# A cubic with one VectorE pass fewer for the offloaded exponentials, with 68 packs instead of 65 and new plan constants, in a gated mix of softmax attention and linear attention

## The chip, the cores and the metric

The kernel runs on one core of one Trainium2 chip. The metric is the device time of one execution in microseconds (us). Most executions of a kernel agree within about 0.3%. Each run also lists the mean clock that TensorE was granted (1.000 is full speed). The *span* is the time from the first to the last instruction of the execution that was profiled.

Engines: PE is TensorE (matmuls), PEld its weight loads, DVE is VectorE, ACT is ScalarE, POOL is GpSimd, SP the engine that issues most transfers.

## The reference

```python
x = A_x                                    # [1, 2048, 512] bf16
g = sigmoid((x * gate_w).sum(-1, keepdims=True))
a = softmax_attention(x, A_wqkv, A_wo)     # 32 heads of 16: softmax(q k^T / 4) v, then @ wo
b = hedgehog_linear_attention(x, B_wqkv, B_w_phi, B_wo)   # features: softmax over 16, of +pq and of -pq
return g * a + (1 - g) * b
```

What costs the time is the softmax attention. It needs exp() of 32 x 2048 x 2048 scores. Four heads' scores of 128 keys by 512 queries are four *units* of 128x512. There are 2048 units.

## The kernel before

The program builds a list of operations with dependences and estimated durations. A scheduler inside the kernel source orders them for each engine, and the result is a fixed instruction order per engine. Changing a constant of the plan changes that order, and with it how many spare matmuls the scheduler puts in to keep TensorE active (103 in before).

The heads are processed in 32 steps (`n`), each of 16 key tiles (`kt`) of four units. ScalarE does the exponentials of most key tiles, out of PSUM into the tile `ET`. Some key tiles, `dve_tiles(n)`, are given to VectorE and GpSimd instead. One such tile is a *pack* of four units, computed with integer tricks and a polynomial.

```python
LEAD = [16.9408, 8.9394, 19.7683, 21.1253, 20.1566]      # plan constants: how early
PACE = [7.9948, 0.4589]                                   # work is released, and when
BOUNDS = [5.8136, 10.5124, 10.0461, 26.2873]              # the linear branch runs
EM = 53
EPHI = 0.49984589
E1, E2, E3 = 125.48413, 43.840203, 9.9574722
DVE_COUNT = (1, 1, 1, 2, 2, 2, 2, 1, 3, 2, 1, 3, 1, 2, 3, 1,      # packs of each step: 65
             2, 3, 2, 2, 2, 2, 3, 2, 1, 3, 2, 2, 4, 1, 3, 3)
# ...
TICK, QUOTA = 3.413, 3700      # spare matmuls keep TensorE active while it has nothing to do
# ...
    def dve_pack(self, n, kt, first_pv):
        # ... four score matmuls into ps_mp, each evacuated by VectorE:
            ws.append(s.op("dve", 0.605, lambda e, i=i, b=b: e.tensor_scalar(
                self.EW[...], self.bk(b), float(EC), float(127 * 65536), op0=ALU.mult, op1=ALU.add), ...))
        # ... integer half on GpSimd, fraction half on VectorE:
        h = s.op("pool", 1.9, lambda e: e.tensor_scalar(
            out().bitcast(dt.int16), half(1, dt.int16), 128.0, float(EM), op0=ALU.mult, op1=ALU.add), ws, ...)
        f = s.op("dve", 1.13, lambda e: e.tensor_scalar(
            self.Ef[:], half(0, dt.uint16), float(2.0 ** -16), -EPHI, op0=ALU.mult, op1=ALU.add), ...)
        t = s.op("dve", 0.6, lambda e: e.tensor_scalar(
            self.Em[:], self.Ef[:], E3, E2, op0=ALU.mult, op1=ALU.add), [f], ...)
        u = s.op("dve", 1.13, lambda e: e.tensor_tensor(self.Em[:], self.Ef[:], self.Em[:], ALU.mult), [t], ...)
        q = s.op("dve", 0.6, lambda e: e.tensor_scalar(self.Em[:], self.Em[:], E1, None, op0=ALU.add), [u], ...)
        g_ = s.op("dve", 1.13, lambda e: e.tensor_tensor(self.Em[:], self.Ef[:], self.Em[:], ALU.mult), [q], ...)
        vs = [s.op("dve", 1.13, lambda e: e.tensor_tensor(out(), out().bitcast(dt.int16), self.Em[:], ALU.add), [g_, h], ...)]
        # ... the pack's four matmuls with V add into the step's accumulator ps_ot
```

Two waits in the main chain tie ScalarE to the packs:

```python
            if ub - NSLOT >= 0:                       # ET has 15 slots: an exponential waits
                deps.append(self.o_pv[(ub - NSLOT) // 4])   # for the matmul that frees its slot
            # ...
                if kt == NT - 1:                      # the step's closing matmul waits for
                    deps += dpv[n]                    # all packs of the step
```

So a pack that comes late delays the closing matmul of its step. The matmuls behind it wait in order, the slots of `ET` fill, and ScalarE stops.

The softmax here doesn't subtract the row's maximum and nothing guards it: scores larger than these inputs give would overflow.

## Time and profile before

| | before |
|---|---|
| time, median of 3 runs | 871.35 us (870.81 to 872.87) |
| span of the profiled run | 871.1 us, granted clock 0.988 |
| ScalarE busy | 842.7 us (97%) |
| VectorE busy | 796.9 us (91%) |
| GpSimd busy | 131.5 us (15%) |

The page gives the busy time of each engine, then the chain of work that ended last, then groups of instructions: line, engine, operation, output<-input, shapes, count, and after the bar the busy time in us, the mean ns of one, and the engine's idle time just before them with what ended most of it. L735 is the exponential on ScalarE. L825 and L828 are the two cheap polynomial passes, L827 a tensor-by-tensor pass.

```profile
PE 748.0 (86%) x5242; PEld 215.5 (25%) x5330; DVE 796.9 (91%) x1118; ACT 842.7 (97%) x783; POOL 131.5 (15%) x76
...
ACT 93%; PE 4%; DVE 1%; SPq 1%; DMA 1%; issue 0%; another core or an unknown queue 0%
...
L735 ACT ACTIVATE ET<-ps_ring 128x1536 bf16<-128x1536 f32 x715 | 817.5, 1346 | 10.8 <-PE ps_ring L718 9.2
...
L827 DVE TENSOR_TENSOR Em<-Ef,Em 128x2048 f16<-128x2048 f16 x65 | 79.3, 1220 | 0.4
...
L825 DVE TENSOR_SCALAR Em<-Ef 128x2048 f16<-128x2048 f16 x65 | 49.2, 757 | 0.4
L828 DVE TENSOR_SCALAR Em<-Em 128x2048 f16<-128x2048 f16 x65 | 47.3, 728 | 0.4
```

ScalarE carries 93% of the chain and VectorE 1%, although VectorE is busy 91% of the span. That is the picture of one bound engine and one that is merely full.

After the head, ScalarE loses time in few places. This is the list of ScalarE's waits in the stretch from 18 to 850 us (total us, times, longest):

```profile
ACT ET L735 <- PE ps_ring L718: 4.3, 4, 1.6
ACT ET L735 <- PE ps_ot L763: 1.4, 2, 1.0
```

The two longest, 1.58 and 1.10 us, follow VectorE's write of `kvbd` at 320.89 us, where the linear branch turns from keys to queries. Lines of the timeline: start, us, engine, line and operation, and in brackets the idle time before it with what ended it.

```profile
320.45 1.90 POOL L819 TENSOR_SCALAR ED<-EW 128x2048 int16<-128x2048 int16 x1 [10.65 <-DVE kvacc L934]
...
320.89 2.00 DVE L938 TENSOR_TENSOR kvbd<-kvacc,m 128x512 bf16<-128x512 f32 x1
...
322.91 1.28 DVE L812 TENSOR_SCALAR EW<-ps_mp 128x512 int32<-128x512 f32 x2
323.65 0.24 PE L990 MATMUL ps_mp<-kvbd,phiT 128*128 128x68 bf16 x2 [1.57 <-DVE EW L812]
...
324.89 5.11 ACT L735 ACTIVATE ET<-ps_ring 128x1536 bf16<-128x1536 f32 x4 [1.58 <-PE ps_ring L718]
```

And the same place by stretches of 4 us (busy time of PE, PEld, DVE, ACT and POOL with instruction counts, then the granted TensorE clock, DMA share and GB/s):

```profile
320.00:324.00 4.00, 2.24 (x15) 0.74 (x16) 4.00 (x7) 3.31 (x4) 1.90 (x1) 0.97 0.05 14
324.00:328.00 4.00, 3.99 (x26) 0.80 (x23) 3.43 (x10) 3.01 (x3) 0.00 (x0) 0.50 0.01 4
328.00:332.00 4.00, 3.64 (x22) 1.10 (x20) 2.83 (x5) 2.84 (x3) 0.00 (x0) 0.68 0.01 2
```

TensorE sits at matmuls that need `kvbd` (L990). The profile puts the end of that wait down to L812, which stood right behind the write on VectorE; either way the write was in front. TensorE's own activity falls (2.24 of 4 us), and ScalarE is fed too slowly.

### The profile page before, as it was taken

What the parts mean: (1) busy time and instruction counts of PE and PEld (TensorE: products, weight loads), DVE (VectorE), ACT (ScalarE), POOL (GpSimd) and SP (SyncE); (2) the same over time, 40 slices, a digit from 0 to 9 for tenths busy, and PEclk for the clock granted to TensorE, in tenths of its full rate; (3) what the DMA queues carried; (4) which work ended last, traced back from release to release, by engine and by line L of the source; (5) the groups of instructions that cost most, each with busy time, mean ns of one, the idle gap of its engine ahead of it and who ended that gap; (6) DMA issues with size and microseconds to landing.
All of it is one profiled execution on the core that took longest, in us unless ns stands there. A gap on an engine that the chain in (4) does not pass through costs nothing.

```text
span 871.1 us, 12869 instructions
## 1 busy us (share of the span) xinstructions
PE 748.0 (86%) x5242; PEld 215.5 (25%) x5330; DVE 796.9 (91%) x1118; ACT 842.7 (97%) x783; POOL 131.5 (15%) x76
## 2 busy tenths in 40 slices
PE   6999998898888888888888888888788897878885
PEld 2323322222222222222222222222222221212221
DVE  2765799999999999979999998999999999999986
ACT  3999999999999999999999999999999999999995
POOL 3000111100110010120102111112100111212020
PEclk8999999999999999999999999999999999999998
DMA  5231000000000000000000000000000000000000
GB/s 109 62 76 52 4 4 3 2 4 5 3 2 4 4 4 8 10 10 10 4 2 9 4 17 9 5 3 2 4 4 10 10 10 8 3 4 4 4 1 25
DMA packets 25115, 11.21 MB, mean 13 GB/s; under 512 B 18016, under 2 KB 25056, under 8 KB 25056
## 3 DMA queue, kind: packets, MB, share of 16 engines
q1 hardware_dynamic: 23472, 9.99, 4.3%
q8 instruction: 42, 0.69, 0.3%
q10 hardware_dynamic: 1584, 0.39, 0.2%
q14 instruction: 17, 0.14, 0.1%
HBM read 3.16 MB, written 2.10 MB: 6 GB/s over the span
## 4 chain that ended last, share of the span: by engine, by line
ACT 93%; PE 4%; DVE 1%; SPq 1%; DMA 1%; issue 0%; another core or an unknown queue 0%
ACT ET L735 90%; ACT phi L958 4%; PE ps_ring L718 2%; PE ps_mp L605 1%; SPq L545 1%; PE ps_ot L763 1%; DMA xT<-in_A_x_dram 0%; DVE kvbd L938 0%; DMA out_dram<-outt 0%; DVE outt L1070 0%; DVE fsum L962 0%; DVE EW L812 0%; PE ps_ot L836 0%; DVE T L847 0%; PE ps_mp L896 0%
## 5 line engine op out<-in xcount | busy, mean ns | idle before, releaser
L735 ACT ACTIVATE ET<-ps_ring 128x1536 bf16<-128x1536 f32 x715 | 817.5, 1346 | 10.8 <-PE ps_ring L718 9.2
L718 PE MATMUL ps_ring<-qT,kT 64*128 64x512 bf16 x1788 | 357.1, 387 | 95.9 <-ACT ET L735 88.9
L819 POOL TENSOR_SCALAR ED<-EW 128x2048 int16<-128x2048 int16 x65 | 124.4, 1915 | 717.4 <-DVE Em L829 101.5
L812 DVE TENSOR_SCALAR EW<-ps_mp 128x512 int32<-128x512 f32 x260 | 170.8, 680 | 11.7 <-PE ps_mp L808 9.0
L763 PE MATMUL ps_ot<-ET,Vaug 128*17 128x512 bf16 x1788 | 176.1, 386 | 1.0 <-ACT ET L735 0.5
L718 PEld LDWEIGHTS ps_ring<-qT,kT 64*128 64x128 bf16 x1788 | 73.7, 93 | 300.2 <-ACT ET L735 260.2
L808 PE MATMUL ps_mp<-qT,kT 128*128 128x512 bf16 x221 | 83.2, 388 | 4.4 <-DVE EW L812 1.0
L822 DVE TENSOR_SCALAR Ef<-EW 128x2048 f16<-128x2048 uint16 x65 | 83.3, 1282 | 0.5
L830 DVE TENSOR_TENSOR ED<-ED,Em 128x2048 uint16<-128x2048 int16 x65 | 81.3, 1251 | 0.5 <-POOL ED L819 0.2
L829 DVE TENSOR_TENSOR Em<-Ef,Em 128x2048 f16<-128x2048 f16 x65 | 81.1, 1247 | 0.5
L827 DVE TENSOR_TENSOR Em<-Ef,Em 128x2048 f16<-128x2048 f16 x65 | 79.3, 1220 | 0.4
L763 PEld LDWEIGHTS ps_ot<-ET,Vaug 128*17 128x17 bf16 x1788 | 43.0, 87 | 141.4 <-issue 129.5
L825 DVE TENSOR_SCALAR Em<-Ef 128x2048 f16<-128x2048 f16 x65 | 49.2, 757 | 0.4
L828 DVE TENSOR_SCALAR Em<-Em 128x2048 f16<-128x2048 f16 x65 | 47.3, 728 | 0.4
L808 PEld LDWEIGHTS ps_mp<-qT,kT 128*128 128x128 bf16 x260 | 24.0, 96 | 64.0 <-issue 31.6
L964 DVE TENSOR_TENSOR phi<-phi,frec 128x1024 bf16<-128x1024 bf16 x32 | 39.2, 1225 | 0.1
L962 DVE TENSOR_REDUCE fsum<-phi 128x64 f32<-128x1024 bf16 x32 | 38.5, 1203 | 0.3 <-ACT phi L958 0.3
L605 PE MATMUL ps_mp<-xT,WA 128*128 128x512 bf16 x110 | 35.5, 388 | 3.7 <-DMA xT<-in_A_x_dram 2.5
L958 ACT ACTIVATE phi<-ps_mp 128x512 bf16<-128x512 f32 x64 | 38.6, 723 | 0.0
L605 PE MATMUL ps_mp<-Wp,xT 128*128 128x512 bf16 x115 | 37.4, 384 | 1.2 <-DVE EW L812 0.5
L662 DVE CAST Vaug<-ps_mp 128x128 bf16<-128x128 f32 (+1 forms) x32 | 13.4, 423 | 17.3 <-PE ps_mp L605 17.1
L847 DVE STREAM_TRANSPOSE T<-ps_ot 128x512 f32<-128x512 f32 x32 | 22.7, 710 | 6.7 <-PE ps_ot L763 6.2
(70 smaller groups left out, 425.7 us busy)
## 6 DMA issues: line engine op xcount, KB each, us to landing
out_dram<-outt SPq DMA_DIRECT2D x16, 128.0 KB, 1.7
qT<-qst SPq DMA_DIRECT2D x120, 16.0 KB, 1.8
WA<-in_A_wqkv_dram SPq DMA_DIRECT2D x3, 384.0 KB, 4.6
WBV<-in_B_wqkv_dram SPq DMA_DIRECT2D x1, 512.0 KB, 4.1
WoA<-in_A_wo_dram SPq DMA_DIRECT2D x1, 512.0 KB, 3.6
WoB<-in_B_wo_dram SPq DMA_DIRECT2D x1, 512.0 KB, 4.3
WA<-in_A_wqkv_dram ACTq DMA_DIRECT2D x3, 128.0 KB, 3.3
xT<-in_A_x_dram SPq DMA_TRANSPOSE x16, 2.7
```

Of the source, the lines that this page charges most:

```text
L605: m = s.op("pe", self.c_mm(n), lambda e, c=c: e.matmul(self.bk(b)[:, 0:n], lhs(c), rhs(c), start=(c == 0), stop=(c == 3)), deps if c == 0 ...
L718: return lambda e: e.matmul(self.ps_ring[:, x % RING, :], self.kT[r, g // 2, kt * P:(kt + 1) * P], self.qT[r, n % 2, i, :], start=True, st ...
L735: self.o_exp.append(s.op("act", w * 0.434 + 0.045, lambda e, b0=b0, s0=s0, w=w: e.activation(self.ET[:, s0:s0 + w, :], self.ps_ring[:, b0: ...
L763: return lambda e: e.matmul(self.ps_ot[32 * i:32 * i + VSL, :], self.Vaug[:, kt, h, :], self.ET[:, (4 * p + k) % NSLOT, :], start=(kt == 0 ...
L808: m = s.op("pe", self.c_mm(512), lambda e, i=i, b=b: e.matmul(self.bk(b), self.kT[:, cp, kt * P:(kt + 1) * P], self.qT[:, n % 2, i, :], st ...
L812: ws.append(s.op("dve", 0.605, lambda e, i=i, b=b: e.tensor_scalar(self.EW[:, ew.idx, i * QCH:(i + 1) * QCH], self.bk(b), float(EC), float ...
L819: h = s.op("pool", 1.9, lambda e: e.tensor_scalar(out().bitcast(dt.int16), half(1, dt.int16), 128.0, float(EM), op0=ALU.mult, op1=ALU.add) ...
L822: f = s.op("dve", 1.13, lambda e: e.tensor_scalar(self.Ef[:], half(0, dt.uint16), float(2.0 ** -16), -EPHI, op0=ALU.mult, op1=ALU.add), ws ...
L827: u = s.op("dve", 1.13, lambda e: e.tensor_tensor(self.Em[:], self.Ef[:], self.Em[:], ALU.mult), [t], pr, port=True)
L829: g_ = s.op("dve", 1.13, lambda e: e.tensor_tensor(self.Em[:], self.Ef[:], self.Em[:], ALU.mult), [q], pr, port=True)
L830: vs = [s.op("dve", 1.13, lambda e: e.tensor_tensor(out(), out().bitcast(dt.int16), self.Em[:], ALU.add), [g_, h], pr, port=True)]
L958: ex.append(s.op("act", 0.478, lambda e, sg=sg: e.activation(self.phi[:, ph.idx, :, sg, :], self.bk(b).rearrange("p (h f) -> p h f", f=DH) ...
```

## The change

Intent: write the cubic about its inflection point. There it has no square term, so it is f·(E3·f² + E1). One VectorE pass per pack goes (the two scalar passes become one, and one product becomes a square). With the room gained, three more packs move from ScalarE to VectorE, and the plan constants are chosen anew. In addition an output block's first matmul waits for all inputs of the block.

```diff
-LEAD = [16.9408, 8.9394, 19.7683, 21.1253, 20.1566]
-PACE = [7.9948, 0.4589]
-BOUNDS = [5.8136, 10.5124, 10.0461, 26.2873]
+LEAD = [16.416095631127316, 9.337289641070926, 19.915460382874, 19.11768171756126, 21.15253173522934]
+PACE = [7.226716164438662, 0.45797175283753105]
+BOUNDS = [5.763727104658085, 10.49730153726035, 10.04197462747977, 27.468332331948613]
 ...
-EM = 53
-EPHI = 0.49984589
-E1, E2, E3 = 125.48413, 43.840203, 9.9574722
+EM = -68
+EU = 0.96498297
+E1, E3 = 61.15205816, 9.99312212
-DVE_COUNT = (1, 1, 1, 2, 2, 2, 2, 1, 3, 2, 1, 3, 1, 2, 3, 1, 2, 3, 2, 2, 2, 2, 3, 2, 1, 3, 2, 2, 4, 1, 3, 3)
+DVE_COUNT = (1, 1, 1, 2, 2, 2, 1, 1, 3, 3, 1, 3, 2, 2, 3, 1, 3, 2, 2, 3, 2, 3, 1, 2, 4, 1, 2, 2, 4, 2, 3, 3)
 ...
-            self.Ef[:], half(0, dt.uint16), float(2.0 ** -16), -EPHI, op0=ALU.mult, op1=ALU.add),
+            self.Ef[:], half(0, dt.uint16), float(2.0 ** -16), EU, op0=ALU.mult, op1=ALU.add),
-        t = s.op("dve", 0.6, lambda e: e.tensor_scalar(
-            self.Em[:], self.Ef[:], E3, E2, op0=ALU.mult, op1=ALU.add), [f], pr, port=True)
-        u = s.op("dve", 1.13, lambda e: e.tensor_tensor(self.Em[:], self.Ef[:], self.Em[:], ALU.mult), [t], pr, port=True)
-        q = s.op("dve", 0.6, lambda e: e.tensor_scalar(self.Em[:], self.Em[:], E1, None, op0=ALU.add), [u], pr, port=True)
+        u = s.op("dve", 1.13, lambda e: e.tensor_tensor(self.Em[:], self.Ef[:], self.Ef[:], ALU.mult), [f], pr, port=True)
+        q = s.op("dve", 0.6, lambda e: e.tensor_scalar(
+            self.Em[:], self.Em[:], E3, E1, op0=ALU.mult, op1=ALU.add), [u], pr, port=True)
 ... (output blocks)
-                    alloc=[b, *also] if k == 0 else (), order=[m], cols=512,
+                    alloc=[b, *also] if k == 0 else (), order=[m] if k else [x[3] for x in bl], cols=512,
```

(The table of tile positions gains a row for five packs, which no step uses.)

More of the change, by code (lines that the diff above doesn't have):

```diff
@@ L28 @@
 PASSES = 1
-LEAD = [16.9408, 8.9394, 19.7683, 21.1253, 20.1566]
-PACE = [7.9948, 0.4589]
-BOUNDS = [5.8136, 10.5124, 10.0461, 26.2873]
+LEAD = [16.416095631127316, 9.337289641070926, 19.915460382874, 19.11768171756126, 21.15253173522934]
+PACE = [7.226716164438662, 0.45797175283753105]
+BOUNDS = [5.763727104658085, 10.49730153726035, 10.04197462747977, 27.468332331948613]
 VSL = 17
 EC = 0.25 * 1.4426950408889634 * 65536
-EM = 53
-EPHI = 0.49984589
-E1, E2, E3 = 125.48413, 43.840203, 9.9574722
-DVE_COUNT = (1, 1, 1, 2, 2, 2, 2, 1, 3, 2, 1, 3, 1, 2, 3, 1, 2, 3, 2, 2, 2, 2, 3, 2, 1, 3, 2, 2, 4, 1, 3, 3)
+EM = -68
+EU = 0.96498297
+E1, E3 = 61.15205816, 9.99312212
+DVE_COUNT = (1, 1, 1, 2, 2, 2, 1, 1, 3, 3, 1, 3, 2, 2, 3, 1, 3, 2, 2, 3, 2, 3, 1, 2, 4, 1, 2, 2, 4, 2, 3, 3)
 def dve_tiles(n):
-    return ((6,), (5, 11), (4, 8, 12), (3, 6, 9, 12))[DVE_COUNT[min(n, NN - 1)] - 1]
+    return ((6,), (5, 11), (4, 8, 12), (3, 6, 9, 12), (2, 5, 8, 11, 13))[DVE_COUNT[min(n, NN - 1)] - 1]
 class Buf:
@@ L1038, in mms @@
                     self.bk(b), src(), W[:, pr, :], start=(k == 0), stop=(k == len(bl) - 1)),
-                    [dep, self.d_woa, self.d_wob], prio, rel, alloc=[b, *also] if k == 0 else (), order=[m], cols=512,
-                    frees=[ba] if ba else ())
+                    [dep, self.d_woa, self.d_wob], prio, rel, alloc=[b, *also] if k == 0 else (), order=[m] if k else [x[3] for x in bl],
+                    cols=512, frees=[ba] if ba else ())
             return m
```

## The prediction

> **What bounds the kernel now.** ScalarE. The page shows ACT busy 842.7 of 871.1 us (97%), and the chain of waits gives it 93% of the span, 90% in the exponentials of the scores (1788 units of 128x512 in 715 instructions). By the table of stretches ACT is busy 50.00 of 50 us nearly everywhere from 150 to 850 us. What it does not cover is the head (first exponential at 14.9 us), the tail (last exponential ends near 861.7), and small stalls: 2.85 us in 300–350 us (TensorE stuck in order behind VectorE's write of kvbd), 1.0 us in 100–150, 0.4 in 50–100. VectorE is busy 796.9 us (91%), about 99% in many stretches, but ACT hardly waits for it: the list of waits has 9.2 us for the exponentials, head included.
>
> **What the change does.** A pack moves four units from ScalarE to VectorE and GpSimd.
> - One VectorE pass a pack goes, and it is the cheap kind: tensor-by-scalar on f16, 757 ns by its group. The three tensor-by-tensor passes (1220 to 1251 ns) stay; one becomes a square of one tile, expected to cost the same. The Trainium skill, "VectorE: DVE Perf Modes", section "Why `tensor_tensor` can't do 2×_2P or 4×", says why the two kinds differ; the trace agrees (757 against 1220–1251 ns at equal size).
> - VectorE per pack: its groups sum to 592.3 us / 65 = 9.11 us; after, 8.35. 68 × 8.35 = 568, so VectorE falls by 24 us to about 773, in spite of three more packs. GpSimd: +3 × 1.9 us, off the path.
> - ScalarE: 12 units fewer. An undisturbed late stretch runs 176 instructions in 198.9 us, 1.130 us per 2.5 units, 0.452 us a unit: 12 × 0.452 = 5.4 us. Exponentials: 817.5 to about 812 us.
> - New constants and the output matmuls' ordering only reorder. The head's TensorE instructions keep their order. Summing VectorE work (trace durations) against ScalarE work over the kernel's 32 steps, after leaves VectorE 10 to 28 us ahead all along, where before ran up to 7 us behind in the middle. So I expect no new starvation.
>
> **On the critical path.** The 24 us of VectorE are off it and become its idle time. Only ScalarE's 5.4 us are on it, in full. The stall at kvbd stays: VectorE's kvbd write still comes right before matmuls that block TensorE, perhaps 0–1.5 us less. I count −0.3 us for all stalls; head and tail unchanged.
>
> 871.35 − 5.4 − 0.3 = **865.6 us**, range 862.8 to 868.6 (8 in 10). Chances: faster by over 2% 0.01; within 2% 0.98; slower by over 2% 0.01. The change is worth about 0.65%.
>
> **What would show each step.** Exponentials 0.457 us busy a unit as now, 12 units fewer. The square 1.20–1.26 us mean; the remaining scalar pass 0.73–0.76. VectorE busy 770–776 us. ACT still full in 150–300 and 350–850 us, its idle time near 28 us; first exponential near 15 us; last exponential to the end 9–10 us.
>
> **What would make it wrong.** (a) A square that reads one tile twice running in a slower mode[...]. (b) The new plan letting TensorE block in order behind a late pack or output block, with new ACT stalls of 1–5 us; or, the other way, removing the kvbd stall (2.85 us) and the early ones (1.4 us): about 862. (c) GpSimd and VectorE holding each other up with three more packs. (d) A lower granted TensorE clock from a thinner matmul stream.

## The result and the profile after

A ratio in this document is the mean time of one kernel's runs over that of the other's of the same rounds. It is therefore not quite the ratio of the medians quoted. The first measurement of the changed kernel gave a median of 863.54 us (862.02 to 864.14, 4 runs) against 871.08 us before. The ratio is 0.9911, with a 95% interval of 0.9896 to 0.9926. By the 2% rule that is "the same", and it is clear of noise.

| | before | after |
|---|---|---|
| median, 4 runs each | 871.08 us | 863.54 us |
| span of the profiled run, clock | 871.1 us, 0.988 | 860.2 us, 0.993 |
| exponentials of scores, busy | 817.5 us, 715 instructions | 811.5 us, 711 instructions |
| ScalarE busy | 842.7 us | 836.7 us |
| VectorE busy | 796.9 us | 784.2 us |
| GpSimd busy | 131.5 us | 138.1 us |

One caution comes first. The two profiles differ by 10.9 us, while the medians differ by 7.5 us. Each profile is of one execution. That of before was the slowest of its four runs (872.87 us), and that of after the fastest of its four (862.02 us).

The page after, the lines that answer to those of before (the square is L825, the scalar pass that is left L826, the product L828):

```profile
PE 742.8 (86%) x5228; PEld 214.7 (25%) x5317; DVE 784.2 (91%) x1080; ACT 836.7 (97%) x779; POOL 138.1 (16%) x79
...
ACT 91%; PE 4%; DVE 3%; DMA 1%; SPq 0%; issue 0%
...
L735 ACT ACTIVATE ET<-ps_ring 128x1536 bf16<-128x1536 f32 x711 | 811.5, 1347 | 5.9 <-PE ps_ring L718 5.5
...
L825 DVE TENSOR_TENSOR Em<-Ef 128x2048 f16<-128x2048 f16 x68 | 87.7, 1290 | 0.6
...
L828 DVE TENSOR_TENSOR Em<-Ef,Em 128x2048 f16<-128x2048 f16 x68 | 86.9, 1278 | 0.3
...
L826 DVE TENSOR_SCALAR Em<-Em 128x2048 f16<-128x2048 f16 x68 | 50.3, 740 | 0.3
```

ScalarE's exponentials took 6.0 us less. VectorE's share of the chain went from 1% to 3%: from 830 us on the chain now runs through the packs.

ScalarE's waits between 18 and 850 us, after:

```profile
ACT ET L735 <- PE ps_ring L718: 0.3, 1, 0.3
```

5.7 us of waits became 0.3 us (of the 5.7, 1.6 lie before 22 us, where the head ends, and 4.1 later). The place where `kvbd` is written, after (timeline, then stretches of 4 us):

```profile
322.00 0.65 DVE L937 TENSOR_TENSOR kvbd<-kvacc,m 128x512 bf16<-128x512 f32 x1
...
323.31 4.76 ACT L735 ACTIVATE ET<-ps_ring 128x1024 bf16<-128x1024 f32 x4
323.49 0.30 PEld L989 LDWEIGHTS ps_mp<-kvbd,phiT 128*128 128x128 bf16 x8 [0.23 <-issue]
...
326.34 1.90 POOL L819 TENSOR_SCALAR ED<-EW 128x2048 int16<-128x2048 int16 x1 [12.64 <-DVE onT_B L1014]
```

```profile
320.00:324.00 4.00, 3.27 (x31) 1.01 (x29) 4.00 (x8) 4.00 (x6) 0.00 (x0) 1.00 0.07 19
324.00:328.00 4.00, 3.58 (x24) 1.15 (x21) 3.93 (x11) 4.00 (x5) 1.66 (x1) 1.00 0.00 0
328.00:332.00 4.00, 4.00 (x31) 0.95 (x31) 4.00 (x6) 4.00 (x5) 0.23 (x1) 1.00 0.00 0
```

The write took 0.65 us instead of 2.00 us. Before, a GpSimd pass that had started 0.44 us earlier ran over it, and the write ended 0.54 us after that pass; after, the GpSimd pass comes 3.7 us later. TensorE was not held up long, the clock stayed at 1.00, and ScalarE was busy 12.00 of 12 us. The Trainium skill, "SBUF — State Buffer", section "SBUF: two separate sides", says that a VectorE instruction with two SBUF inputs and a GpSimd instruction that reads SBUF exclude each other on a shared pair of ports. This agrees: the `kvbd` write has two SBUF inputs and took 2.00 us beside a GpSimd pass and 0.65 us without one.

### The profile page after: what moved, and what is told of

It is laid out like the page before. It is cut to its first block, busy times and chain, and to the rows that moved or that the text cites. A ratio compares the mean times of both kernels' runs of the same rounds, so it can differ in the third digit from the quotient of the medians. Undisturbed runs are those within 1.5% of the kernel's fastest.

```text
span 860.2 us, 12805 instructions
## 1 busy us (share of the span) xinstructions
PE 742.8 (86%) x5228; PEld 214.7 (25%) x5317; DVE 784.2 (91%) x1080; ACT 836.7 (97%) x779; POOL 138.1 (16%) x79
## 4 chain that ended last, share of the span: by engine, by line
ACT 91%; PE 4%; DVE 3%; DMA 1%; SPq 0%; issue 0%
ACT ET L735 87%; ACT phi L957 4%; PE ps_ring L718 2%; PE ps_mp L1036 1%; PE ps_mp L605 1%; DVE EW L812 1%; PE ps_ot L763 1%; SPq L545 0%; DVE ED L829 0%; DVE Ef L822 0%; DMA xT<-in_A_x_dram 0%; DVE Em L828 0%; DVE T L851 0%; DVE Em L825 0%; DVE qT L623 0%
## 5 line engine op out<-in xcount | busy, mean ns | idle before, releaser
L735 ACT ACTIVATE ET<-ps_ring 128x1536 bf16<-128x1536 f32 x711 | 811.5, 1347 | 5.9 <-PE ps_ring L718 5.5
L718 PE MATMUL ps_ring<-qT,kT 64*128 64x512 bf16 x1775 | 352.8, 385 | 92.7 <-ACT ET L735 82.9
L819 POOL TENSOR_SCALAR ED<-EW 128x2048 int16<-128x2048 int16 x68 | 131.0, 1927 | 702.7 <-DVE Em L828 78.5
L812 DVE TENSOR_SCALAR EW<-ps_mp 128x512 int32<-128x512 f32 x272 | 177.8, 679 | 20.9 <-PE ps_mp L808 11.5
L825 DVE TENSOR_TENSOR Em<-Ef 128x2048 f16<-128x2048 f16 x68 | 87.7, 1290 | 0.6
L822 DVE TENSOR_SCALAR Ef<-EW 128x2048 f16<-128x2048 uint16 x68 | 87.5, 1286 | 0.6
L828 DVE TENSOR_TENSOR Em<-Ef,Em 128x2048 f16<-128x2048 f16 x68 | 86.9, 1278 | 0.3
L826 DVE TENSOR_SCALAR Em<-Em 128x2048 f16<-128x2048 f16 x68 | 50.3, 740 | 0.3
L835 PE MATMUL ps_ot<-ED,Vaug 128*17 128x512 bf16 x272 | 26.7, 383 | 0.4 <-DVE ED L829 0.3
L605 PE MATMUL ps_mp<-WA,xT 128*128 128x128 bf16 (+1 forms) x128 | 23.0, 278 | 1.9 <-DVE kT L652 0.6
```

The lines of the kernel that those rows point to most:

```text
L605: m = s.op("pe", self.c_mm(n), lambda e, c=c: e.matmul(self.bk(b)[:, 0:n], lhs(c), rhs(c), start=(c == 0), stop=(c == 3)), deps if c == 0 ...
L718: return lambda e: e.matmul(self.ps_ring[:, x % RING, :], self.kT[r, g // 2, kt * P:(kt + 1) * P], self.qT[r, n % 2, i, :], start=True, st ...
L735: self.o_exp.append(s.op("act", w * 0.434 + 0.045, lambda e, b0=b0, s0=s0, w=w: e.activation(self.ET[:, s0:s0 + w, :], self.ps_ring[:, b0: ...
L819: h = s.op("pool", 1.9, lambda e: e.tensor_scalar(out().bitcast(dt.int16), half(1, dt.int16), 128.0, float(EM), op0=ALU.mult, op1=ALU.add) ...
L822: f = s.op("dve", 1.13, lambda e: e.tensor_scalar(self.Ef[:], half(0, dt.uint16), float(2.0 ** -16), EU, op0=ALU.mult, op1=ALU.add), ws + ...
```

## The experiments

Theory: ScalarE's units are the time (0.452 us each), and stalls that the new order of work removed are the rest. The pass taken off VectorE has no value in itself; it pays for the packs. Rivals: VectorE's load holds the kernel up even before; or the plan makes the gain and the units do not; or the ordering of output matmuls does.

All twelve kernels gave correct results. Each was timed over five rounds beside the kernel before on the same chip; "n" is the number of runs.

| run | what it is | median us (range, n) | ratio to before (95%) |
|---|---|---|---|
| ctl_before | before | 870.87 (870.73–871.74, 5) | 1.0000 (0.9989–1.0012) |
| ctl_after | after | 865.20 (862.11–866.78, 6) | 0.9923 (0.9908–0.9939) |
| cubic_old_plan | before + cubic only | 870.48 (868.19–872.32, 6) | 0.9991 (0.9977–1.0005) |
| after_old_counts | after with 65 packs | 872.74 (868.37–874.16, 6) | 1.0008 (0.9986–1.0030) |
| quartic_new_plan | after with the old polynomial | 897.19 (892.51–898.06, 5) | 1.0284 (1.0262–1.0306) |
| after_old_order | after, old output ordering | 865.25 (862.56–867.46, 6) | 0.9928 (0.9910–0.9946) |
| after_70 | after with two packs more | 874.15 (872.49–874.84, 6) | 1.0027 (1.0011–1.0042) |
| after_quota5000 | after, more spare matmuls | 862.76 (860.90–866.64, 6) | 0.9912 (0.9888–0.9936) |
| before_62 | before with three packs fewer | 880.45 (877.55–882.90, 6) | 1.0106 (1.0087–1.0126) |
| before_new_constants | before, new constants only | 907.24 (906.08–908.41, 4) | 1.0414 (1.0397–1.0430) |
| after_old_counts_q | 65 packs, more spare matmuls | 870.32 (867.67–872.20, 6) | 0.9986 (0.9969–1.0002) |
| after_69_q | 69 packs, more spare matmuls | 872.91 (871.98–873.73, 5) | 1.0018 (1.0005–1.0032) |

### Two controls

Edit: none.

> The kernel before, unchanged, as a control and a second profile of it. Every theory: ratio 1.000, interval about 0.002 wide on either side, 870 to 873 us. What it tells is the spread: the profiled execution of before had 4.1 us of ScalarE stalls after the head (2.7 us of it at the write of kvbd, which took 2.0 us there, and 1.4 us near 92 and 100 us) and was the slowest of its four. If these stalls belong to the plan, the second profile has them too (3.5 to 4.5 us). If they were that execution's bad luck, it has under 2 us of them and a span near 868.5.

> The changed kernel, unchanged, for five more times and a second profile. Ratio 0.991 (0.9896 to 0.9926 is on record). The first profile had no ScalarE stall at all from 18 us to the end and was the fastest of its four (862.0 us); the three others were 1 to 2 us longer. If that is stalls that come and go, the second profile shows 0.5 to 2 us of ScalarE idle time in the stretches after 50 us; if it is the head, the first exponential starts 0.5 to 2 us later than 15.2 us.

Measured: before repeats at a ratio of 1.0000, and its second profile has the same stalls at the same places: 1.4 us near 91 and 100 us at full clock, and 2.8 us after the `kvbd` write, which again took 2.00 us. These belong to the plan of before; they are not bad luck.

The changed kernel's second profile was of its slowest run (866.78 us, clock 0.986). It has no stall near 91 to 100 us and none at `kvbd`, where the write again took 0.65 us. It has others, which the first profile lacked. In stretches of 4 us, the second profile of the changed kernel:

```profile
72.00:76.00 4.00, 4.00 (x70) 2.09 (x66) 2.28 (x5) 4.00 (x5) 0.00 (x0) 0.93 0.04 12
76.00:80.00 4.00, 4.00 (x31) 1.15 (x29) 0.52 (x3) 3.19 (x5) 0.00 (x0) 0.50 0.00 0
80.00:84.00 4.00, 4.00 (x22) 1.18 (x21) 1.62 (x3) 2.63 (x3) 0.00 (x0) 0.72 0.00 0
...
424.00:428.00 4.00, 2.84 (x18) 0.62 (x18) 4.00 (x10) 4.00 (x5) 0.00 (x0) 0.88 0.06 16
428.00:432.00 4.00, 4.00 (x23) 1.24 (x21) 0.97 (x3) 3.05 (x4) 1.90 (x1) 0.70 0.00 0
```

ScalarE loses time in these stretches, where the granted clock is at a half for all or part of the time (at 72 and 424 us it does not yet). In the first profile of the same instruction order the clock was 1.00 in these stretches and ScalarE was full. So with one and the same order of work, the execution decides whether an episode of half clock comes. That the order of work sets where it *can* come is only suggested: the profiles of after_old_order and after_69_q have an episode at 420 to 428 us too (clocks of 0.75 and 0.82, and of 0.83 and 0.75). The Trainium skill, "TensorE: Matmul & The Clock Gate", section "Part 1: The HAM clock gate (the "warmup" mystery)", says that the clock is full or half by the activity in a window of about 3.4 us that runs freely and does not start with the kernel. The trace agrees in the half (0.50). A free-running window would explain why the same program meets it at different places; that it does so here is argued from the page, not shown by a run.

What the runs do show is that the clock goes with the time. Within the five runs of ctl_before (which have two clocks only, 0.990 and 0.992) and the six of ctl_after, time and mean clock have a correlation of −1.00, with a slope of 0.47 and 0.65 us per 0.001 of clock (a straight line fitted to each kernel's runs). That does not show which of the two drives the other. The changed kernel's runs go from 862.11 us at 0.993 to 866.78 us at 0.986.

### The cubic alone

Edit to before: the polynomial, nothing else.

```diff
+EM = -68; EU = 0.96498297; E1, E3 = 61.15205816, 9.99312212     # and the five-pass body; 65 packs, old constants
```

> The cubic with one pass fewer alone: old pack counts (65), old constants, old ordering of the output matmuls. My theory (VectorE is off the critical path, the time is ScalarE's units): ScalarE does the same 1788 units, so 869.5 to 871.5 us, ratio 0.998 to 1.000, while VectorE's busy time falls by 40 to 46 us to about 755. Rival (VectorE's load itself holds the kernel up, through late buffers and a blocked TensorE): 4 us or more of gain from this alone, ratio 0.995 or less, with the ScalarE stalls gone.

Measured: 870.48 us, ratio 0.9991, and the interval includes 1. The pass alone is worth nothing measurable. VectorE's busy time fell to 769.7 us, a fall of 27 us, not the 40 to 46 I expected. The traces account for the miss. The pass gone is 65 × 0.683 us (its median), 44.4 us. Those VectorE instructions that overlap a GpSimd pass and last at least 0.3 us longer than the median of their line run over that median by 28.3 us in all, against 20.4 us in the profile of before, so 7.9 us more. The other 9.3 us are the difference between sums of groups and busy time (explained with the prediction below).

The page of this run:

```profile
PE 768.6 (88%) x5348; PEld 217.5 (25%) x5348; DVE 769.7 (89%) x1053; ACT 842.4 (97%) x783; POOL 130.8 (15%) x76
```

This profile also shows that the stall at `kvbd` needs no new constants to go away: the write took 0.69 us with no GpSimd pass over it, and ScalarE was busy 16.00 of 16 us from 308 to 324 us. Nothing was gained by it. The 1.4 us near 91 and 100 us stayed, and ScalarE lost 2.8 us in two episodes of lower clock near 79 and 381 us (stretches at 0.62, and at 0.50 and 0.65): 4.2 us after the head, as before. VectorE's load was not on the critical path of the kernel before.

### The packs undone

Edit to after: the old `DVE_COUNT`.

```diff
-DVE_COUNT = (1, 1, 1, 2, 2, 2, 1, 1, 3, 3, ...)   # 68
+DVE_COUNT = (1, 1, 1, 2, 2, 2, 2, 1, 3, 2, ...)   # 65
```

> The changed kernel with only the old pack counts put back: 65 packs, 1788 units, new constants, new ordering, cubic. My theory: the 12 units come back to ScalarE at 0.452 us, so 5.4 us longer than the changed kernel: 868 to 870 us, ratio 0.997, and what is left of the gain (about 2 us) is the stalls that the new order of work took away. Rival (the gain is the plan and the order of work, not the units): within 2 us of the changed kernel, ratio 0.991 to 0.993.

Measured: a median of 872.74 us, which is 7.5 us longer than the changed kernel beside it and outside my 868 to 870. Two of its six runs had a clock of 0.992 and took 868.4 and 868.9 us; four had 0.983 to 0.987 and took 872.1 to 874.2 us. So I repeated the comparison with more spare matmuls in both kernels:

```diff
-    TICK, QUOTA = 3.413, 3700
+    TICK, QUOTA = 3.413, 5000
```

> The changed kernel with a higher quota of spare matmuls (5000 columns in each 3.413 us instead of 3700), which does no useful work and only keeps TensorE active. The two profiles of the changed kernel differ by 4.8 us of span; the longer one had the granted clock at a half in two more episodes (72 to 83 us and 424 to 431 us) and 3.4 us of ScalarE stalls inside these two. If the clock makes the spread, more spare matmuls give a clock of 0.992 or more and 862 to 863.5 us, ratio 0.990, with a narrower spread. If the spread has another cause, time and spread stay (862 to 867 us).

> The changed kernel with the old pack counts (as before: 872.7 us median, 868.4 to 874.2, four of its six runs at a clock of 0.983 to 0.987) and with the higher quota of spare matmuls. If the clock made it 7.5 us rather than 5.4 us longer than the changed kernel, the clock rises to 0.990 or more and the time falls to 867 to 869.5 us, ratio 0.996 to 0.998. If its work is slower for another reason, it stays near 872 us.

(The 3.4 us of stalls named in the first of these two texts are 3.1 us by the stretches shown under the controls.)

Measured: 862.76 us with 68 packs and 870.32 us with 65. More spare matmuls did not do what I expected of them: the changed kernel's range stayed wide (860.90 to 866.64 us), and its ratio of 0.9912 cannot be told from the 0.9923 and 0.9911 without. The kernel with 65 packs came down from 872.74 to 870.32 us, just outside the range I gave. So the quota is no cure.

The two profiles, however, happen to be a clean pair. From the pages, first with 68 packs, then with 65:

```profile
PE 795.5 (92%) x5592; PEld 223.8 (26%) x5592; DVE 784.2 (91%) x1080; ACT 836.8 (97%) x779; POOL 138.1 (16%) x79
L735 ACT ACTIVATE ET<-ps_ring 128x1536 bf16<-128x1536 f32 x711 | 811.6, 1347 | 6.7 <-PE ps_ring L718 6.3
```

```profile
PE 781.2 (90%) x5603; PEld 225.4 (26%) x5696; DVE 769.9 (89%) x1053; ACT 842.2 (97%) x783; POOL 131.0 (15%) x76
L735 ACT ACTIVATE ET<-ps_ring 128x1536 bf16<-128x1536 f32 x715 | 817.1, 1351 | 6.7 <-PE ps_ring L718 6.3
```

Both have only the stalls of the head (6.3 us of waits for scores in each) and clocks of 0.993 and 0.992. ScalarE is busy 836.8 us with 68 packs and 842.2 us with 65. The difference is 5.4 us, which is 12 units at 0.452 us, and the spans differ by 6.1 us (861.0 and 867.1). That settles the main term: the three packs are worth 5.4 us of ScalarE time, and all of it reaches the span. (The other 0.7 us of the pair is not explained.)

All runs together say the same once the clock is taken out. I read each kernel's straight line of time over clock at 0.991. Before then takes 871.2 to 871.4 us in its three sets, the cubic alone 870.0, after with 65 packs 869.4 (869.5 with more spare matmuls), and after 863.3 (864.2 with more spare matmuls). So the packs are worth 6.1 us, and 5.3 in the second pair, and all the rest of the change under 2 us. Without this correction the two kernels with 65 packs, at ratios of 1.0008 and 0.9986, gained nothing that these runs resolve: none of the measured gain is there without the packs. (The correction also takes out what a kernel itself does to its clock, so it is an aid to reading and not a second measurement.)

### Three packs fewer in the kernel before

```diff
 DVE_COUNT: one pack fewer in the ninth, eighteenth and twenty-ninth step (62 packs)
```

> The kernel before with three packs fewer (62 instead of 65: one fewer in the ninth, eighteenth and twenty-ninth step), nothing else. ScalarE does 1800 units instead of 1788, VectorE about 25 us less. My theory (time is ScalarE's units at 0.452 us): 5.4 us longer than before, 875.5 to 877.5 us, ratio 1.006. Rival (VectorE's load holds before up): no longer than before, or shorter, ratio 1.000 or less.

Measured: 880.45 us, ratio 1.0106. The direction refutes the rival: taking VectorE work away made the kernel longer. The size is 9 us rather than 5.4. ScalarE's exponentials were busy 823.1 us, 5.6 us more than in the profile of before. Part of the rest goes with more episodes of lower clock: the profile has three of them between head and tail where that of before has one, and the six runs have clocks of 0.982 to 0.991. Read at a clock of 0.991 as above, the kernel takes 878.2 us, 6.8 us more than before, so about 1.4 us are neither units nor clock. Six tenths of the excess are the units; the plan was not tuned for 62 packs.

### The old polynomial under the new plan

Edit to after: the old polynomial with its extra pass; 68 packs and all else as in after.

> The changed kernel's plan (68 packs, new constants, new ordering) with the old polynomial, so one VectorE pass a pack more: 68 times 0.7 us, 48 us. ScalarE does the same 1776 units as the changed kernel. My theory: the pass buys the room for the packs, and VectorE, at 48 to 50 of 50 us in most stretches of the changed kernel, has at most 30 us of room between 100 and 850 us, so ScalarE is held up for 10 to 25 us: 873 to 890 us, ratio 1.003 to 1.022, with new ScalarE waits after 100 us. Rival (the pass does not matter at this load, the plan does): 863 to 866 us, ratio 0.991 to 0.994.

Measured: 897.19 us, ratio 1.0284, worse than I expected. ScalarE's waits over the whole run:

```profile
ACT ET L735 <- PE ps_ot L763: 23.7, 11, 7.0
```

The longest of these waits, in the timeline (the pack's last VectorE pass, its matmul, the matmul behind it, ScalarE):

```profile
804.37 1.22 DVE L830 TENSOR_TENSOR ED<-ED,Em 128x2048 uint16<-128x2048 int16 x1
...
805.64 0.39 PE L836 MATMUL ps_ot<-ED,Vaug 128*17 128x512 bf16 x4 [2.98 <-DVE ED L830]
...
805.87 0.39 PE L763 MATMUL ps_ot<-ET,Vaug 128*17 128x512 bf16 x4
806.31 2.37 ACT L735 ACTIVATE ET<-ps_ring 128x1536 bf16<-128x1536 f32 x2 [7.00 <-PE ps_ot L763]
```

This is the chain that the code predicts for a late pack: TensorE waits for the pack, the next matmul that frees a slot of `ET` waits behind it, and ScalarE stands 7.00 us. The same pass that is worth nothing at 65 packs is worth 32 us at 68 (897.19 against the changed kernel's 865.20, measured in another set of runs on another chip; after_old_order, in the same set, took 865.25).

### The ordering of the output matmuls

Edit to after: `order=[m]` put back for the first matmul of a block.

> The changed kernel with only the ordering of the output matmuls put back. If that ordering keeps TensorE from blocking inside an output block, putting it back costs stalls: 1 to 3 us longer than the changed kernel's 864.5, ratio 0.9935 to 0.996. My guess is that it does little: within 1 us, ratio 0.991 to 0.9935.

Measured: 865.25 us, ratio 0.9928, against 0.9923 and 0.9911 for the changed kernel. Within what these runs resolve, the ordering is worth nothing.

### The new constants alone

Edit to before: `LEAD`, `PACE` and `BOUNDS` of after.

> The kernel before with only the new plan constants (lead times, pace and bounds), old polynomial, 65 packs, old ordering. Both profiles of before have a ScalarE stall of 1.4 us near 91 and 100 us at full clock and of 2.7 us at the write of kvbd; profiles of the changed kernel have neither. If the constants alone took these away: 1 to 4 us shorter, ratio 0.9955 to 0.999. If it needs the cheaper pack as well, the constants alone give 0 or a loss, ratio 1.000 or more.

Measured: 907.24 us, ratio 1.0414. I had thought of a gain or of a small loss. The constants suit the whole plan only. Here the profile has waits of ScalarE of up to 17.8 us behind late packs, and in one of them the engines stood behind each other in their fixed orders. A stretch of 50 us and one line of the list of waits from 795 to 866 us:

```profile
800.00:850.00 50.00, 41.78 (x279) 10.87 (x281) 22.34 (x30) 45.56 (x41) 3.80 (x2) 0.95 0.01 2
```

```profile
DVE T L847 <- PE ps_ot L763: 26.0, 1, 26.0
```

VectorE was busy 22.34 of 50 us because a transpose stood first in its queue and waited 26.0 us for the end of a step, while the packs that the later steps needed stood behind it.

### More packs than 68

```diff
 DVE_COUNT: after_70: third step 1 -> 2, thirtieth 2 -> 3;  after_69_q: twenty-eighth step 2 -> 3, QUOTA = 5000
```

> The changed kernel with two packs more (70, 1768 units; one more in the third step and one more in the thirtieth). My theory of ScalarE units at 0.452 us: 3.6 us shorter than the changed kernel, 860 to 862 us, ratio 0.988. Rival (VectorE and TensorE are full by now, the plan has no room left): no gain or a loss, 864 us or more, with ScalarE waits in the stretches 75 to 125 us or 740 to 850 us.

> The changed kernel with the higher quota of spare matmuls and one pack more (69), in the twenty-eighth step, where the profile of the changed kernel shows VectorE at 45.8 of 50 us. If there is room for one pack there: 1.8 us shorter than the kernel with the quota alone (862.8), near 861 us, ratio 0.989. If the plan is full (two packs more, elsewhere, cost 9 us): 863 to 868 us, with ScalarE waits after 720 us.

Measured: 874.15 and 872.91 us. Against the changed kernel's 865.20 and the 862.76 of the one with the higher quota, they lost 9 and 10 us where the units would have saved 3.6 and 1.8. The waits of ScalarE for matmuls with V, which the profile of after does not have at all, first in after_70, then in after_69_q:

```profile
ACT ET L735 <- PE ps_ot L763: 10.1, 7, 4.4
```

```profile
ACT ET L735 <- PE ps_ot L763: 10.2, 5, 7.3
```

In both they lie mostly between 750 and 850 us, where ScalarE's busy time falls to 41.8 to 49.0 of 50 us. after_70 also loses time near 76 to 104 us, part of it at half clock, and its tail after the last exponential is 13.2 us long where that of after is 9.5. No version here beats the changed kernel beyond noise. I did not retune the constants for either, so this shows that the plan as it stands is full; it does not show that 68 is a limit.

## Why the prediction was right

The prediction was 865.6 us with a range of 862.8 to 868.6. The first measurement was 863.54 us; the second, with six runs, 865.20 us. Point by point:

- **ScalarE bounds, and the 12 units are worth 5.4 us in full: right.** ScalarE's exponentials took 6.0 us less in the first pair of profiles. In the clean pair with and without the three packs ScalarE was busy 5.4 us less, and the span was 6.1 us shorter. At equal clock the runs give 5.3 and 6.1 us.
- **The saved VectorE time is off the critical path: right, with the limits that the prediction missed.** The cubic alone gave a ratio of 0.9991. But at 68 packs the same pass decides: with it back the kernel took 897 us. The prediction called the saving idle time. It is the room that the three packs need, and under these constants nothing is left of it: one pack more cost 10 us, two more 9 us.
- **The square costs a tensor-by-tensor pass: right.** Its median is 1215 ns, as that of the products (1214 to 1215 ns); the mean of 1290 ns lies above my 1.20 to 1.26 us because of passes that overlap GpSimd. The same goes for the removed pass: I took 757 ns, its mean in before; its median is 683 ns. The Trainium skill, "VectorE: DVE Perf Modes", section "The perf-mode tier table (the rule you actually need)", gives 693 ns for the scalar kind and 1224 ns for the tensor-by-tensor kind at 2048 elements of bf16. These medians, on f16, agree within 2%. Not every tensor-by-scalar pass is cheap: the first of a pack, L822, reads every second 16-bit value and has a median of 1217 ns.
- **VectorE busy 770 to 776 us: wrong, 784.2.** My sum was a fall of 24.3 us; it was 12.7. The packs' groups sum to 572.5 us, not 568 (4.5 us of the miss). All other groups rose by 1.3 us. The remaining 5.8 us come from setting sums of groups against the engine's busy time: the groups of before sum to 864.7 us and those of after to 846.1, while the busy time counts overlapping parts of back-to-back instructions once.
- **Stalls worth 0.3 us, "the stall at kvbd stays": wrong, and this is the term that was mis-sized.** In both profiles of before the stalls after the head that belong to the plan are 4.1 to 4.2 us (1.4 us near 91 and 100 us, 2.7 to 2.8 us at `kvbd`). In both profiles of after these are gone. ScalarE's idle time, foretold as near 28 us, fell from 28.4 us in the first profile of before to 23.5 us in the first of after. The prediction had named this case itself, under (b) of what would make it wrong. I looked at the order of instructions only. I did not see that a GpSimd pass lay over the `kvbd` write, nor that the stall continued at half clock. Not all of the 4 us is kept: the slower executions of the changed kernel have new episodes of half clock elsewhere. Beyond the 5.4 us of units, the means of the two sets (863.3 against 871.3, and 864.8 against 871.1) leave 2.6 and 0.9 us. In the second profile of after ScalarE's idle time is 27.7 us again. So it is partly luck that the second median, 865.20 us, lies within 0.4 us of the forecast: stalls that the prediction kept were gone, and episodes of half clock that it did not have took most of the gain back.
- **"New constants only reorder": too light.** Reordering alone, without the cheaper pack and the counts, cost 4.1%.
- **"After leaves VectorE 10 to 28 us ahead all along": misleading.** It was a running sum that carries idle time of the head forward as if it could be spent later. after_69_q and after_70 put it to the test and found no such room.

What stays open: what makes the clock drop in one execution and not in the next, what of the gain beyond the units (under 2 us at equal clock) belongs to the constants and what to the cheaper pack, and whether another set of constants would let 69 packs pay. The changed kernel's gain is between 0.8% and 0.9%, depending on how many episodes of half clock its runs meet.

## What to carry to other kernels

Work saved on an engine that is full but not critical is worth nothing until it is spent on moving work off the critical engine. Price it by what it lets you move, and test that it was needed by putting it back under the new plan. Parts of a jointly tuned plan do not add up: here one part alone gave nothing, another alone cost 4%, and together they gave 0.8 to 0.9%. When a difference is below one per cent, compare several executions and their granted clocks before you read a story out of one pair of profiles.

## What the Trainium skill lacked or had wrong

- "TensorE: Matmul & The Clock Gate" says that busyness in a window sets the clock. Busy time as a profile shows it is no guide to it here: in the second profile of after TensorE is shown busy 4.00 of 4 us from 68 to 76 us, in part with one-column matmuls, and the clock went to 0.50 directly after. The page has no figure for how much activity within the window is enough.
- The same page speaks of variation from run to run only for the warm-up, whose penalty it puts under 1% of a typical kernel. I found no page that says that executions of one already warm kernel differ by it in mid-run: here 0.5 to 0.7 us per 0.001 of mean clock, and 862.1 to 866.8 us for one kernel.
- "VectorE: DVE Perf Modes" gives durations of undisturbed instructions, which the medians meet (683 and 1215 ns). It does not warn that means in a trace contain waits for GpSimd (the block itself is described in "SBUF — State Buffer"): 757 ns by the mean against 683 by the median for the removed pass, and 20 to 28 us of such waits in all, by my count.
